# ScalarE's first-layer order pinned anew, and one weight group begun before the state sums, in a gated delta rule with a GELU layer pair

## The chip, the cores and the metric

The kernel runs on one core of a Trainium2 chip. Its engines are TensorE (PE: matrix products, and PEld: loading their weights), VectorE (DVE), ScalarE (ACT), GpSimd (POOL) and SyncE (SP, which issues most DMAs). The metric is the time of one execution on the device in microseconds; lower is better.

## The reference

The work is a delta rule over 768 positions, for 4 x 8 heads of 48, whose output is the input of two dense layers with an exact GELU between them. All arrays are float32, but `moe_w_in` and `moe_w_out` arrive as float64, which the kernel decodes itself.

```python
B, H, S, D = q.shape                      # 4, 8, 768, 48
k_n = k / (norm(k, axis=-1) + 1e-6)
for t in range(S):
    y[:, :, t] = q_t @ state
    v_old = state^T k_t
    state = state + beta_t * outer(k_t, v_t - v_old)
x = y.transpose(0, 2, 1, 3).reshape(B * S, H * D)      # 3072 x 384
h = x @ w_in                                           # 384 x 2048
g = 0.5 * h * (1 + erf(h / sqrt(2)))
out = g @ w_out                                        # 2048 x 384
```

## The kernel before

**Tiling.** The positions are cut into 12 chunks of 64. Within a chunk the recurrence is a triangular system, so that the state is touched once per chunk. A unit is one chunk of one pair of batches (`NA` = 2 units a chunk, 128 partitions: 2 batches x 64 positions, 8 heads). Two chunks make a group; its triangular systems are eliminated together on VectorE (`eliminate_steps`) and joined on TensorE (`join`, from the third chunk on `join_run`). A chunk then goes: products with the state (`against_state`, psK), `subtract` (VectorE makes W, ScalarE copies y), `solve` (psU, ScalarE copies U), `use` and `update` (psY and psS), `next_state` (VectorE adds psS to the state St), `read` (x), `turn` (x transposed, xT).

**The two layers.** `fc1(c, f)` makes one of 16 slices of the hidden layer of chunk c: three products into a PSUM tile psH (L784), then a GELU on ScalarE into G. For chunk 0 psH takes one of two buffers (tag "mlp"), so slice f + 2 waits until the GELU of slice f has read its own. `fc2` makes psO from G and w_out (L802). From chunk 2 on other forms of both layers are used, which the change does not touch.

**Decoding the weights.** A float64 weight comes as two 32-bit words. `w_in` is 8 groups (0 to 7) of 256 columns, `w_out` 8 more (8 to 15). For group n: `fetch` (three or two DMAs from SP into a staging buffer), `begin` (VectorE takes the exponent bits out, L231 or L234), `exponents` (ScalarE maps them: two Prelu instructions where `two_kinks`, among these groups 3 to 7, else one Relu; L237, or L875 where they go through `keep`), `mantissas` (VectorE, L251 and L253), `signed` (VectorE, L261, and L260 where there is one kink), which also issues the fetch of the group four (w_in) or three (w_out) further on. Slice f of the first layer needs group f // 2.

**What sets the order.** The beginning, up to `by_hand.close()`, is written in program order for all engines. It ends with group 2's decoding and `next_state` of chunk 0. The rest is a list of steps with marks: `plan` gives each step a number, `emit` calls them in the order of these numbers. In this part VectorE executes in exactly that order. On the other engines a scheduler places an instruction where it reckons it ready, except that instructions that went through `keep` (which records them at its own line, L875) keep the program's order among themselves. For chunk 0 the GELUs go through `keep`, and so do the exponents of groups 3 to 7 (`decode_in`); slice f has its mark at 1.0 + 0.031 (f + 0.5), about. `decode_in` gives each group four marks: begin, exponents, mantissas, signed.

**The squares.** `sum_of_squares(u, h)` squares the 48 key values of one head on ScalarE and adds them up in the same instruction (L328; the trace shows it as two records). There are 32, for chunks 2 and 3, with marks from 1.48 to 1.8. They do not go through `keep`. In the order that the scheduler makes of it, three of them stand before the first exponents of group 3 and the others between the exponents and GELUs of the first layer. GpSimd then takes the square root of the sums as a power (`prep`, L349), one instruction for each of the two chunks, and VectorE makes factors of them (`finish_both`, L301 to L305) once the weights are decoded, as the first step of the second group's elimination. ScalarE also scales V with the roots (`scale_head`, L371).

Of the kernel before, what the change touches and what calls it, by code (L numbers as in the profile page):

```python
# [15 lines left out]
ACT = mybir.ActivationFunctionType  # L16
# [3 lines left out]
def kernel(  # L20
# [28 lines left out]
    nc = tc.nc  # L49
    B, H, S, D = q.shape  # L50
# [52 lines left out]
    for c in range(NC):  # L103
        for a in range(NA):
            u = tiles[c, a] = Unit()
# [96 lines left out]
    def fetch(n):  # L202
        if n >= len(w_parts):
            return
        dst, src = w_parts[n]
        if n < n_in:
            raw = stage[:, n % NS * 2 * WG:(n % NS + 1) * 2 * WG]
        else:
            raw = slots[(n - n_in) % len(slots)]
        w_raw[n] = raw.rearrange("q (n w) -> q n w", w=2)  # L210
        raw = raw.rearrange("q (m n w) -> q m n w", m=dst.shape[1], w=2)
        for m in range(dst.shape[1]):
            nc.sync.dma_start(out=raw[:, m], in_=src[:, m])
# [4 lines left out]
    def two_kinks(n):  # L218

        return 2 < n < n_in or n > n_in and n % 2 == 0  # L220

    def high(e, dt):

        return e.bitcast(dt).rearrange("q (n w) -> q n w", w=2)[:, :, 1]

    def begin(n):
        e = su.tile([128, WG], U32, tag="w_e", name="w_e")
        raw = w_raw.pop(n)
        halves[n] = w_parts[n][0].rearrange("q m n -> q (m n)"), raw[:, :, 0], raw[:, :, 1], e
        if two_kinks(n):  # L230
            nc.vector.tensor_scalar(e.bitcast(I32), raw[:, :, 1].bitcast(I32), 20, -1,  # L231
                                    op0=ALU.arith_shift_right, op1=ALU.bitwise_and)
        else:
            nc.vector.tensor_scalar(e, raw[:, :, 1], 20, 0x7FF, op0=ALU.logical_shift_right,  # L234
                                    op1=ALU.bitwise_and)
# [12 lines left out]
    def mantissas(n):  # L248
        dst, lo, hi, e = halves[n]
        bits = dst.bitcast(U32)  # L250
        nc.vector.tensor_scalar(bits, hi, 0xFFFFF, 0x100000, op0=ALU.bitwise_and,  # L251
                                op1=ALU.bitwise_or)
        nc.vector.scalar_tensor_tensor(dst, lo, 2.0 ** -32, bits, ALU.mult, ALU.add)  # L253

    def signed(n):

        dst, lo, hi, e = halves.pop(n)
        scale = high(e, BF16) if two_kinks(n) else e.bitcast(F32)
        if not two_kinks(n):
            nc.vector.scalar_tensor_tensor(e, hi, 0x80000000, e, ALU.bitwise_and, ALU.bitwise_or)  # L260
        nc.vector.scalar_tensor_tensor(dst, dst, 2.0 ** -20, scale, ALU.mult, ALU.mult)  # L261
        after = n + (NS if n < n_in else len(slots))
        if (after < n_in) == (n < n_in):
            fetch(after)
# [12 lines left out]

    def decode_in():

        marks = {3: (0.986, 0.988, 0.99, 1.07), 4: (1.05, 1.06, 1.1, 1.155),  # L280
                 5: (1.14, 1.15, 1.19, 1.22), 6: (1.205, 1.215, 1.25, 1.28),
                 7: (1.265, 1.27, 1.33, 1.36)}
        steps = []
        for n, (a, b, c, d) in marks.items():
            steps += [(a, (begin, n)), (b, (exponents, n, keep)), (c, (mantissas, n)), (d, (signed, n))]
        return steps

    NW = len(w_parts)
# [2 lines left out]
    Ds, Gs, Nus, XMs, gms, ns = {}, {}, {}, {}, {}, {}  # L291
# [28 lines left out]
    def sum_of_squares(u, h):  # L320

        if "both" not in ns:
            n23 = wk.tile([128, 2 * NA, H], F32, tag="n0", name="n0", bufs=1)
            ns[2], ns[3] = n23[:, 0:NA], n23[:, NA:]
            ns["both"] = n23
        if h == 0:
            u.ksq = wk.tile([128, H, D], F32, tag="ksq", name="ksq", bufs=1)
        nc.scalar.activation(u.ksq[:, h], u.Kn[:, h, 0:D], ACT.Square,  # L328
                             accum_out=ns[u.c][:, u.a, h:h + 1])

    def norms(c):
        us = [tiles[c, a] for a in range(NA)]
# [386 lines left out]
    def next_state(u):  # L719
        if u.c < NC - 1:  # L720
            nc.vector.tensor_tensor(St[:, u.a], St[:, u.a], u.psS, op=ALU.add)
# [152 lines left out]
    def keep(fn, *args, **kw):  # L874
        tc.keep_in_program_order(fn(*args, **kw))  # L875
# [254 lines left out]
    exponents(2)  # L1130
    mantissas(2)
    signed(2)
    for u in first[:NA]:
        next_state(u)
    by_hand.close()
# [16 lines left out]
    def state_at(c, *times, first=(), second=()):  # L1152

        steps = state_steps(c, first, second)
        if len(times) > len(steps):
            steps = steps[:-1] + [(turn, tiles[c, a]) for a in range(NA)]
        return [(t, step) for t, step in zip(times, steps) if t is not None]

    plan = [at(c + 1 + 0.25 * (c == 1), c + 2 + 0.25 * (c == 0), ffn_steps(c)) for c in range(NC)]
    plan += [decode_in(), at(1.365, 1.9, decode_steps(n_in, NW)), at(1.91, 1.911, [(1.0, late)])]  # L1160
    rows1, join1 = eliminate_steps(1), join_steps(1)
    plan += [at(0.98, 0.985, [(1.0, load, 3)]),
             [(t, (join, 0, range(NA, 2 * NA), level)) for level, t in enumerate((1.085, 1.16))],
]
    sums = [(1.0, sum_of_squares, tiles[c, a], h) for c in (2, 3) for a in range(NA) for h in range(H)]
    plan += [at(1.48, 1.8, sums), at(1.81, 1.811, [(1.0, fn, c) for c in (2, 3) for fn in (norms, prep)]), at(1.9, 1.905, [(1.0, finish_both)]), at(2.725, 2.726, [(1.0, queries, third)]),
             state_at(1, 1.31, 1.4, 1.5, 1.56, 1.58),
# [125 lines left out]
```

## Time and profile before

| what | value |
|---|---|
| runs, us | 649.33, 651.1, 651.32 (median 651.1) |
| the profiled execution, us | 652.12 |
| its span, first to last instruction, us | 650.4 |
| mean granted TensorE clock | 0.981 |
| PE busy | 623.0 us, 96%, 9702 instructions |
| DVE busy | 499.4 us, 77%, 1023 instructions |
| ACT busy | 259.2 us, 40%, 586 instructions |
| POOL busy | 63.3 us, 10%, 58 instructions |
| one square, two records on ACT, ns | 230 and 188 (median), overlapping |
| one power on POOL, ns | 2914 (mean) |
| w_in DMAs from 54 to 72 us, issue to landing, us | 3.1 to 4.9, median 4.1 |

Times in the texts are microseconds from the start of the span, unless said otherwise. A timeline row gives start, duration, engine, line, operation, output <- inputs, shape, and in brackets the idle time of the engine before it and what ended that. "x6" is six records; a float32 product of TensorE shows as two records, so one slice of the first layer is six. A stage row gives the stretch, its length, then busy time (and records) of PE, PEld, DVE, ACT and POOL, the mean granted TensorE clock, the DMA engines' busy share, and GB/s. A busy TensorE is not TensorE at its peak[...].

### The profile page before, as it was taken

The page shows a single profiled execution, that of the slowest core. Times are in us where ns is not written, and L with a number is a line of the kernel's source. Part 1 is how long each engine was busy: PE and PEld are TensorE (multiplying, and loading weights), DVE is VectorE, ACT ScalarE, POOL GpSimd, SP SyncE. Part 2 cuts the span into 40 slices and gives each one's busy share as a digit, 9 for nine tenths or more (in the row PEclk, how much of TensorE's full clock was granted, in tenths as well). Part 3 has the DMA queues.
Part 4 walks back from the last instruction along what each step waited for, and adds up shares of the span by engine and source line. Part 5 has one row for each costly group of instructions (what it writes and reads, how often), then busy time and mean ns, then how long its engine had stood idle before and what let it go on. Part 6 is the DMA issues. An engine that isn't in the chain of part 4 may idle for free.

```text
span 650.4 us, 22163 instructions
## 1 busy us (share of the span) xinstructions
PE 623.0 (96%) x9702; PEld 575.8 (89%) x9702; DVE 499.4 (77%) x1023; ACT 259.2 (40%) x586; POOL 63.3 (10%) x58
## 2 busy tenths in 40 slices
PE   6767999999999999999999999999999999999997
PEld 5665777776799999999999999999999999999997
DVE  6999579998899997999767999667999665454342
ACT  3366875723453147133147133157133153132230
POOL 4042110100121003101003001004001000000000
PEclk9976799999999999999999999999999999999999
DMA  9795727211543235222325312312222400100101
GB/s 128 173 274 167 128 75 220 24 25 30 87 64 48 42 50 93 43 40 38 65 27 85 60 31 38 67 17 44 38 31 35 71 6 3 25 2 2 26 2 25
DMA packets 158433, 39.79 MB, mean 61 GB/s; under 512 B 150016, under 2 KB 153216, under 8 KB 158336
## 3 DMA queue, kind: packets, MB, share of 16 engines
q1 hardware_dynamic: 155344, 36.94, 29.8%
q10 hardware_dynamic: 2992, 1.43, 1.0%
q8 instruction: 76, 1.25, 0.8%
q14 instruction: 21, 0.17, 0.1%
HBM read 33.62 MB, written 4.72 MB: 59 GB/s over the span
## 4 chain that ended last, share of the span: by engine, by line
PE 83%; DVE 10%; ACT 3%; DMA 2%; issue 2%; SPq 0%; DVEq 0%; ACTq 0%
PE psX L832 12%; PE psY L887 11%; PE psY L832 8%; PE psX L887 8%; PE psO L802 6%; PE psV L887 5%; PE psZ L887 5%; PE psH L784 5%; PE psZ L832 4%; PE psV L832 4%; PE psK L658 3%; PE psG L412 3%; PE psJ L584 2%; DVE tmp L492 2%; DVE Nu L494 2%; PE psY L707 2%
## 5 line engine op out<-in xcount | busy, mean ns | idle before, releaser
L494 DVE TENSOR_TENSOR Nu<-Nu,tmp 128x30 f32<-128x30 f32 (+9 forms) x180 | 61.3, 341 | 6.2
L887 PE MATMUL psX<-xT,w_in_sb 128*128 128x128 f32 x480 | 64.6, 277 | 0.6 <-DVE p L984 0.5
L492 DVE TENSOR_TENSOR tmp<-Nu 128x30 f32<-128x30 f32 (+9 forms) x180 | 61.1, 340 | 4.7
L887 PEld LDWEIGHTS psX<-xT,w_in_sb 128*128 128x128 f32 x480 | 58.8, 192 | 2.0 <-issue 0.8
L875 ACT COPY xT<-psX 128x768 f32<-128x768 f32 x9 | 7.2, 798 | 124.4 <-PE psX L761 124.4
L832 PE MATMUL psX<-w_out_sb,G 128*128 128x192 f32 x320 | 55.3, 326 | 0.0
L784 PE MATMUL psH<-xT,w_in_sb 128*128 128x256 f32 x192 | 47.2, 401 | 5.1 <-ACT G L875 5.1
L832 PEld LDWEIGHTS psX<-w_out_sb,G 128*128 128x128 f32 x320 | 52.1, 190 | 0.0
L349 POOL TENSOR_TENSOR n<-n,half 128x16 f32<-128x16 f32 x10 | 29.1, 2914 | 230.4 <-DVE n L347 203.1
L784 PEld LDWEIGHTS psH<-xT,w_in_sb 128*128 128x128 f32 x192 | 37.6, 200 | 12.8 <-ACT G L875 6.7
L802 PE MATMUL psO<-w_out_sb,G 128*128 128x384 f32 x128 | 44.5, 493 | 0.0
L887 PE MATMUL psY<-xT,w_in_sb 128*128 128x128 f32 x320 | 42.3, 275 | 0.0
L875 ACT COPY pu<-psZ 128x512 f32<-128x512 f32 x40 | 23.4, 586 | 39.1 <-PE psZ L887 39.1
L887 PEld LDWEIGHTS psY<-xT,w_in_sb 128*128 128x128 f32 x320 | 38.9, 192 | 0.0
L802 PEld LDWEIGHTS psO<-w_out_sb,G 128*128 128x128 f32 x128 | 23.4, 190 | 14.1 <-DVE w_out_sb L261 0.5
L875 ACT ACTIVATE G<-G 128x512 f32<-128x512 f32 x40 | 25.2, 629 | 19.0 <-DVE G L918 18.1
L374 POOL TENSOR_TENSOR V<-V,n 128x384 f32<-128x384 f32 x18 | 16.6, 936 | 133.3 <-DMA V<-in_v_dram 55.4
L832 PE MATMUL psZ<-T,pu 128*128 128x192 f32 x160 | 28.6, 332 | 0.0
L832 PE MATMUL psY<-T,G 128*128 128x192 f32 x160 | 28.6, 332 | 0.0
L910 DVE TENSOR_TENSOR psY<-psY,pu 128x512 f32<-128x512 f32 x20 | 14.0, 698 | 18.0 <-PE psY L887 18.0
L832 PE MATMUL psV<-w_out_sb,G 128*128 128x192 f32 x160 | 27.7, 326 | 0.0
L832 PE MATMUL psX<-T,G 128*128 128x192 f32 x160 | 27.6, 326 | 0.0
(179 smaller groups left out, 1348.4 us busy)
## 6 DMA issues: line engine op xcount, KB each, us to landing
Kp<-in_k_dram SPq DMA_DIRECT2D x76, 96.0 KB, 3.4
w_out_sb<-in_moe_w_in_dram SPq DMA_DIRECT2D x24, 256.0 KB, 4.5
w_raw<-in_moe_w_out_dram SPq DMA_DIRECT2D x16, 384.0 KB, 5.2
V<-in_v_dram SPq DMA_DIRECT2D x48, 96.0 KB, 3.3
out_dram<-o_sb SPq DMA_DIRECT2D x36, 96.0 KB, 2.2
Qp<-in_q_dram SPq DMA_DIRECT2D x64, 32.0 KB, 2.3
Qp<-in_q_dram SPq DMA_DIRECT2D x16, 96.0 KB, 4.4
Qp<-in_k_dram SPq DMA_DIRECT2D x32, 32.0 KB, 2.4
```

The source lines that it names most:

```text
L349: nc.gpsimd.tensor_tensor(flat, flat, half, op=ALU.pow)
L374: engine.tensor_tensor(u.V, u.V, ns[u.c][:, u.a].unsqueeze(2).to_broadcast([128, H, D]), op=ALU.mult)
L412: nc.tensor.matmul(psG[HALF[p], r, i * NP + j, :], lhsT=u.Kt[rows, p, j, :], rhs=(u.Qt if x else u.Kt)[rows, p, j, :], start=True, stop=True)
L492: nc.vector.tensor_tensor(tmp, nu[:, j + 1:, j:j + 1].to_broadcast([128, n, j]), nu[:, j:j + 1, 0:j].to_broadcast([128, n, j]), op=ALU.mult)
L494: nc.vector.tensor_tensor(nu[:, j + 1:, 0:j], nu[:, j + 1:, 0:j], tmp, op=ALU.add)
L658: nc.tensor.matmul(u.psK[to, x, r, j, :], lhsT=(u.Qt if x else u.Kt)[rows, p, j, :], rhs=St[rows, u.a, p ^ r, j, :], start=True, stop=True)
L784: nc.tensor.matmul(psH, lhsT=w_in_sb[:, f // 2, m, f % 2 * 128:(f % 2 + 1) * 128], rhs=xTs[c][:, m, :], start=(m == 0), stop=(m == NM - 1))
L802: nc.tensor.matmul(u.psO, lhsT=G[:, u.a, f, :], rhs=w_out_sb[:, f, :], start=(f == 0), stop=(f == NF - 1))
L832: nc.tensor.matmul(ps_, lhsT=lhs[:, f, :], rhs=rhs[:, f, :], start=first and f == 0, stop=f == FH - 1, skip_group_check=not first)
L875: tc.keep_in_program_order(fn(*args, **kw))
L887: nc.tensor.matmul(ps_[:, i], lhsT=lhs[:, f // 2, f % 2 * 128:(f % 2 + 1) * 128], rhs=rhs, start=first and i == 0, stop=True, skip_group_c ...
L910: nc.vector.tensor_tensor(L1["Y1"], L1["Y1"], L1["pu"][:, 0], op=ALU.add)
```

## The change

Three edits, with no instruction added or removed.

1. `decode_in` has other marks. Exponents of groups 3 to 7 move to 1.03, 1.09, 1.18, 1.24 and 1.30, which puts each pair between two GELUs: after slice 0, 2, 5, 7 and 9. Before they stood at 0.988, 1.06, 1.15, 1.215 and 1.27: before slice 0, and after slices 1, 4, 6 and 8. Some begin, mantissas and signed marks move too.
2. `begin(3)` leaves that list and is called by hand after `signed(2)`, ahead of `next_state` of chunk 0, whose two additions to the state follow it on VectorE.
3. `sum_of_squares` goes through `keep`: the 32 squares keep their place in the program, behind the GELUs of chunk 0.

```diff
     def decode_in():
 
-        marks = {3: (0.986, 0.988, 0.99, 1.07), 4: (1.05, 1.06, 1.1, 1.155),
-                 5: (1.14, 1.15, 1.19, 1.22), 6: (1.205, 1.215, 1.25, 1.28),
-                 7: (1.265, 1.27, 1.33, 1.36)}
+        marks = {3: (None, 1.03, 0.99, 1.04), 4: (1.0, 1.09, 1.1, 1.13),
+                 5: (1.12, 1.18, 1.14, 1.2), 6: (1.19, 1.24, 1.21, 1.25),
+                 7: (1.245, 1.3, 1.29, 1.36)}
         steps = []
         for n, (a, b, c, d) in marks.items():
-            steps += [(a, (begin, n)), (b, (exponents, n, keep)), (c, (mantissas, n)), (d, (signed, n))]
+            if a is not None:
+                steps += [(a, (begin, n))]
+            steps += [(b, (exponents, n, keep)), (c, (mantissas, n)), (d, (signed, n))]
         return steps
...
-        nc.scalar.activation(u.ksq[:, h], u.Kn[:, h, 0:D], ACT.Square,
-                             accum_out=ns[u.c][:, u.a, h:h + 1])
+        keep(nc.scalar.activation, u.ksq[:, h], u.Kn[:, h, 0:D], ACT.Square,
+             accum_out=ns[u.c][:, u.a, h:h + 1])
...
     exponents(2)
     mantissas(2)
     signed(2)
+    begin(3)
     for u in first[:NA]:
         next_state(u)
     by_hand.close()
```

## The prediction

> **What bounds the kernel now.** I read the page first, then the waits between 58 and 98 us, the stage table (`busy of each engine by stretch`), and the timelines of TensorE and ScalarE there. On the page TensorE's row of slices reads 9 from the fifth slice (65 us) on. That hides two things in the start, up to 97 us: waits between slices, and products that are busy at half the clock.
>
> The timelines of the two engines in the first layer of chunk 0, TensorE first:
>
> ```profile
> 59.73 1.89 PE L784 MATMUL psH<-xT,w_in_sb 128*128 128x256 f32 x8
> 65.36 2.24 PE L784 MATMUL psH<-xT,w_in_sb 128*128 128x256 f32 x6 [3.75 <-ACT G L875]
> 67.53 1.92 PE L539 MATMUL psJ<-XM,G 32*32 32x32 f32 x64
> 69.38 4.59 PE L784 MATMUL psH<-xT,w_in_sb 128*128 128x256 f32 x12
> ...
> 75.03 2.86 PE L784 MATMUL psH<-xT,w_in_sb 128*128 128x256 f32 x12
> ```
>
> ```profile
> 62.21 0.94 ACT L875 ACTIVATE w_e<-w_e,lim 128x768 f32<-128x768 int32 x1 [3.23 <-DVE w_e L231]
> ...
> 63.27 1.14 ACT L875 ACTIVATE w_e<-w_e,lim 128x768 int16<-128x768 f32 x1
> ...
> 64.95 0.36 ACT L875 ACTIVATE G<-psH 128x256 f32<-128x256 f32 x1
> ```
>
> The first product (6 records, f = 0) is finished near 59.9, yet its GELU runs at 64.95: the two exponents of group 3 are pinned in front of it, and ScalarE waits 3.23 us for the begin of that group on VectorE. The third product needs the PSUM buffer that this GELU frees, so TensorE stands 3.75 us. The two rows of 12 records are the same work, 4.59 us and 2.86 us. The stage table says why: after the stall the granted clock (eighth column, PEclk) is 0.55.
>
> ```profile
> 61.50:65.40 3.90, 0.15 (x2) 0.04 (x1) 3.53 (x6) 3.19 (x13) 0.00 (x0) 1.00 0.99 251
> 65.40:73.00 7.60, 7.60 (x79) 6.01 (x80) 3.41 (x7) 5.39 (x29) 3.03 (x1) 0.55 0.89 163
> 73.00:97.20 24.20, 22.84 (x456) 18.66 (x454) 17.74 (x26) 19.86 (x61) 2.92 (x2) 1.00 0.37 82
> 97.20:119.00 21.80, 21.80 (x92) 15.37 (x92) 21.38 (x29) 10.84 (x20) 0.00 (x0) 1.00 0.57 164
> ```
>
> The waits from 58 to 98 us, who waited for whom, in total, times, longest:
>
> ```profile
> PE psH L784 <- ACT G L875: 5.1, 4, 3.7
> DVE XM L550 <- PE psJ L539: 4.1, 1, 4.1
> ...
> ACT w_e L875 <- DVE w_e L231: 3.2, 1, 3.2
> DVE w_in_sb L261 <- ACT w_e L875: 2.7, 3, 1.4
> ```
>
> So ScalarE's order holds both others: TensorE loses 5.1 us standing and 7.6 x 0.45 = 3.4 us to the clock; VectorE waits 4.1 us for the late join and 2.7 us for exponents that stand behind squares. From 97.2 on TensorE has no gap (21.80 of 21.80).
>
> [...] 3.75 us idle, then clock near 0.5 for some 7 us. [...] the trace has a ready GELU behind a waiting exponent. [...] The trace is mixed: L253 took 1.47 instead of 0.96 us beside GpSimd's V product (50.19 to 52.33), but 0.96 beside the power at 69.97. [...]
>
> **The change part by part.** The built order of both kernels differs in few places. SP's and GpSimd's queues are the same, item by item: no DMA is issued in another order. VectorE: begin of group 3 stands before the two state sums; group 7's mantissas before the W block (four instructions) instead of behind it. ScalarE: each GELU and each pair of exponents in the order of the marks; the 32 squares behind the first layer; the exponent of group 9 now before the six copies of U. TensorE: one or two small products moved.
>
> *Begin of group 3 earlier* costs nothing in work. 0.5 us (L231: 0.55) go before the sums, which end at 62.2 instead of 61.7. Behind them waits the join's PSUM buffer, wanted at 62.9. Its weights were fetched at 31 to 35 us, so it does not wait itself.
>
> *The order and the squares.* I replay the trace by hand, each instruction starting when its engine and its inputs are ready. Durations, start to start, from rows at full clock: product 1.56 (6 records), join 1.1, psK 2.0, psU 1.1, psY 2.1; VectorE L231 0.47, L251 0.59, L253 0.88, L261 0.88, so mantissas 1.47, join scaling 1.41, W block 2.1; ScalarE GELU 0.26 to 0.36, exponents 0.94 and 1.1 (2.0 a pair), Zf copies 1.1, U copies 1.95, square 0.225.
> TensorE: f = 0 ends 59.9, f = 1 61.3. GELU 0 runs at 60.1, so f = 2 starts at 61.3: the stall is gone, and with it the slow clock. Join 62.9 to 64.0, f = 3 and 4 to 67.1, join to 68.2, f = 5 to 9 to 76.0, psK to 78.0, f = 10 and 11 to 81.1. The GELUs free each buffer in time (GELU 6 at 72.6 for f = 8 at 72.9 is the tightest).
> VectorE: begin 3 at 60.7, sums to 62.15, mantissas 3 to 63.6, begin 4 to 64.1, signed 3 to 65.0 (exponents done 63.3), join scaling 66.4, mantissas 4 67.9, begin 5 68.3, signed 4 69.2, mantissas 5 70.7, begin 6 71.2, signed 5 73.1 (its exponents end at 72.2, behind the Zf copies and GELU 5), mantissas 6 74.6.
> Here the fetch of group 7 is late: it is issued by SP from 69.68 to 71.8, behind twelve other loads, in an order that does not change; its three DMAs landed 3.7 to 3.8 us after issue, so about 75.2. Begin 7 to 75.7, signed 6 76.6, mantissas 7 78.1, W block 80.2, signed 7 81.1, begin 8 81.6.
> ScalarE: y copies to 80.3 behind W, GELU 10 80.6, so f = 12 from 81.2 to 82.8, psU 83.9, f = 13 and 14 to 87.0. The exponent of group 9 waits for begin 9 (83.5), ends 84.5, then U to 86.45 and GELU 13 86.75. This pin puts U back by 0.6 us (psU is ready at 83.9), which f = 13 and 14 hide. f = 15 runs 87.0 to 88.5, psY 88.5 to 90.6: TensorE has no gap worth naming left.
> The second layer (psO) then starts at 90.6. Before it starts at 97.21: **6.6 us** earlier. With a landing of 4.9 us, the longest of the twelve w_in DMAs, begin 7 moves 1.1 us and the same chain gives 5.5. I take 6.1, the middle.
>
> *After that.* TensorE is dense to 160 us, so what arrives earlier ends earlier, if VectorE's decoding of w_out and ScalarE keep up. Both chains hang on psS and x, which move by the same amount. The 32 squares, 32 x 0.225 = 7.2 us, now lie here. ScalarE had gaps of 0.97, 1.11, 1.44, 1.60 and 1.93 us before its instructions from 100 to 111 us; by the built order the squares come as 2, 5, 6, 7, 6, then 5 and 1: 0.45, 1.1, 1.35, 1.6, 1.35 us. They fit, to 0.1. The five ahead of the second GELU of chunk 1 make it 1.2 us late, which costs TensorE about 0.15 through a PSUM buffer. The last square ends near 108.6, the power on GpSimd 2.9 us later at 111.6, and VectorE wants it at 119.03 - 6.6 = 112.4. I cost them at nothing; with that cover gone they cost up to 1 us. Beside the two powers L253 may stretch by 0.5 us each; the row at 69.97 shows none. Both ends stay in the range.
>
> **Sum.** The span goes from 650.4 to 644.3; the profiled execution took 652.12 (1.7 around the span), so 646.0. The median of the runs is 651.1, 1.0 below it; the same 6.1 us gives 645.0.
>
> **The rivals.** *Half the gain.* The clock falls anyway: TensorE still works in pieces in the 60s[...]. Against it: the replay leaves no gap over 0.3 us before 80. Price: the 3.4 us above; 651.1 - 6.1 + 3.4 = 648.4.
> *Slower.* The squares move ScalarE's work into the stretch where VectorE is the full engine (21.38 of 21.80 us from 97.2 to 119), each w_out group waiting for its exponent. If the 7.2 us fall in whole on that chain, and TensorE on it, the end is 651.1 - 6.1 + 7.2 = 652.2. It turns slower when more than 6.1 us of the squares, 28 of 32, stand before exponents already wanted. For it: the groups of squares fit the gaps to 0.1 us. Against: they do fit, and VectorE's next step hangs on an exponent only at L260 and L261.
> *Nothing.* The gain comes at 90.6 and is lost before 160, for TensorE has other work to fill in and a later chain (VectorE's elimination from 119, back to back) ends last: 651. Against: that chain starts from the decoding, which moves too.
>
> **How the numbers follow.** Forecast 0.78 (643.5 to 646.8: the terms 5.5 and 6.6, up to 1 us for squares and powers, and 1 us for the spread of the runs, 649.33 to 651.32). Half the gain 0.09, nothing 0.06, slower 0.07. About 0.3%, 2 us, is what a measurement of this kernel can tell from no change. Faster 0.87, within 0.06, slower 0.07. The range goes from 643.0 to 648.6, to take in the half gain.
>
> **What would show it.** Right: no wait of TensorE for a GELU over 1 us from 58 to 90; clock 1.0 from 60 on; the joins at about 63 and 67 (before 67.5 and 73.9); begin 7 as the first VectorE instruction that waits for a DMA; psO first at 90 to 92; then every row to 160 earlier by the same 6 us. Wrong: a clock of 0.5 after 62; VectorE waiting at L260 or L261 for exponents from 95 to 112; the factors (L301 of before) waiting for GpSimd; or a shift at psO that is gone at 160.

## The result, and the profile after

| | kernel before | kernel after |
|---|---|---|
| median of 18 runs each, us | 649.9 | 646.12 |
| the profiled execution, us | 652.12 | 647.82 |
| its span, us | 650.4 | 645.8 |
| median of the spans, us | 648.6 (41 runs, of the second measurement) | 644.1 (18 runs) |
| time outside the span, us | 1.7 | 2.0 |

The ratio of the means is 0.9944, with a 95% interval from 0.993 to 0.9958: 3.6 us faster (3.8 between the medians). One slow run of before, of 1246.54 us, is left out of the ratio. A second measurement gave 0.9926 (0.9906 to 0.9946). The prediction was 645.0, in a range from 643.0 to 648.6: right in the sign and the range, 1.1 us too low. The gain that it forecast was 6.1 us.

The timelines of TensorE, then ScalarE, in the kernel after (lines are two higher than before, so L786 is the first layer's product, L804 the second layer's, L877 `keep`):

```profile
57.64 4.53 PE L786 MATMUL psH<-xT,w_in_sb 128*128 128x256 f32 x18
62.10 1.20 PE L541 MATMUL psJ<-XM,G 32*32 32x32 f32 x64
63.23 2.86 PE L786 MATMUL psH<-xT,w_in_sb 128*128 128x256 f32 x12
66.02 1.20 PE L541 MATMUL psJ<-Zf,XM 32*32 32x32 f32 x64
67.15 7.14 PE L786 MATMUL psH<-xT,w_in_sb 128*128 128x256 f32 x30
...
80.55 1.56 PE L786 MATMUL psH<-xT,w_in_sb 128*128 128x256 f32 x6 [0.86 <-ACT G L877]
...
86.89 1.56 PE L786 MATMUL psH<-xT,w_in_sb 128*128 128x256 f32 x6 [0.92 <-ACT G L877]
...
90.40 1.56 PE L804 MATMUL psO<-w_out_sb,G 128*128 128x384 f32 x4
```

```profile
59.62 0.38 ACT L877 ACTIVATE G<-psH 128x256 f32<-128x256 f32 x1 [1.97 <-PE psH L786]
60.52 2.13 ACT L877 ACTIVATE w_e<-w_e,lim 128x768 f32<-128x768 int32 x2 [0.51 <-DVE w_e L231]
62.51 0.63 ACT L877 ACTIVATE G<-psH 128x256 f32<-128x256 f32 x2
```

Slices 0, 1 and 2 now stand in one row of 18 records without a wait for a GELU. Their first GELU runs at 59.62, as soon as its product is there, and the exponents of group 3 come behind it. The same stretches in the stage table (busy of PE, PEld, DVE, ACT and POOL, then the granted clock):

```profile
61.50:65.40 3.90, 3.90 (x78) 3.27 (x77) 3.80 (x7) 3.50 (x5) 0.00 (x0) 1.00 1.00 219
65.40:73.00 7.60, 7.47 (x93) 6.10 (x92) 6.93 (x11) 6.17 (x12) 0.00 (x0) 1.00 0.75 162
73.00:97.20 24.20, 22.31 (x400) 17.61 (x400) 19.69 (x30) 18.01 (x56) 0.00 (x0) 1.00 0.57 138
97.20:119.00 21.80, 21.76 (x84) 15.48 (x83) 20.93 (x36) 18.41 (x79) 8.57 (x3) 1.00 0.41 108
```

TensorE is busy for 3.90 us of the first stretch, against 0.15, and the clock is 1.00 in the second, against 0.55. The waits between 58 and 98 us:

```profile
PE psH L786 <- ACT G L877: 1.8, 2, 0.9
DVE w_e L231 <- DMA w_out_sb<-in_moe_w_in_dram: 1.5, 1, 1.5
...
DVE w_in_sb L261 <- ACT w_e L877: 0.5, 1, 0.5
```

TensorE's waits for GELUs fall from 5.1 to 1.8 us, VectorE's for exponents from 2.7 to 0.5, and its wait of 4.1 for the join is gone. A new one stands between them: VectorE waits 1.5 us for a DMA.

In the kernel before, the second layer's first row is:

```profile
97.14 1.56 PE L802 MATMUL psO<-w_out_sb,G 128*128 128x384 f32 x4
```

It now starts at 90.40, 6.7 us earlier, and VectorE's rows at 160 us are 6.8 earlier. About 0.6 of that was there before the change's place: VectorE's last step of group 2 stood at 59.05 against 59.70. At the end, only 4.6 is left, for between 162 and 168 the profiled execution of after lost 2.2 us again. The pause of TensorE there, and two windows (a window, here and below, is a stretch of 3.41 us; the changes of the granted clock in that profile lie on its edges):

```profile
163.57 0.43 PE L718 MATMUL psY<-U,Kp 64*64 64x48 f32 x11 [1.34 <-issue]
```

```profile
160.84:164.25 3.41, 1.79 (x73) 1.51 (x66) 3.31 (x8) 1.55 (x3) 1.67 (x1) 1.00 0.35 44
164.25:167.66 3.41, 3.41 (x7) 1.69 (x6) 2.63 (x6) 0.00 (x0) 1.23 (x1) 0.50 0.43 54
```

TensorE pauses 1.34 us in the middle of chunk 2's state update (for nothing that the profile names), is busy for 1.79 of 3.41 us, and gets half the clock for the next 3.41. Whether that belongs to the change was the first question.

### The profile page after: what moved, and what is told of

Same layout as the page of the kernel before. It is cut to its first block, busy times and chain, and to the rows that moved or that the text cites. A ratio compares the mean times of both kernels' runs of the same rounds, so it can differ in the third digit from the quotient of the medians.

```text
span 645.8 us, 22160 instructions
## 1 busy us (share of the span) xinstructions
PE 621.7 (96%) x9702; PEld 574.4 (89%) x9702; DVE 499.2 (77%) x1023; ACT 260.3 (40%) x586; POOL 63.4 (10%) x58
## 3 DMA queue, kind: packets, MB, share of 16 engines
q10 hardware_dynamic: 2992, 1.43, 1.1%
## 4 chain that ended last, share of the span: by engine, by line
PE 86%; DVE 8%; ACT 2%; issue 2%; DMA 1%; ACTq 0%; SPq 0%; DVEq 0%
PE psX L834 12%; PE psY L889 11%; PE psX L889 8%; PE psY L834 7%; PE psO L804 7%; PE psH L786 6%; PE psV L889 5%; PE psZ L889 5%; PE psZ L834 4%; PE psV L834 4%; PE psK L660 3%; PE psG L414 3%; PE psJ L586 2%; DVE tmp L494 2%; DVE Nu L496 2%; PE psU L690 2%
## 5 line engine op out<-in xcount | busy, mean ns | idle before, releaser
L877 ACT COPY xT<-psX 128x768 f32<-128x768 f32 x9 | 7.2, 799 | 124.3 <-PE psX L763 124.3
L804 PE MATMUL psO<-w_out_sb,G 128*128 128x384 f32 x128 | 46.4, 508 | 0.0
L786 PE MATMUL psH<-xT,w_in_sb 128*128 128x256 f32 x192 | 44.6, 386 | 1.9 <-ACT G L877 1.8
L786 PEld LDWEIGHTS psH<-xT,w_in_sb 128*128 128x128 f32 x192 | 36.1, 192 | 8.7 <-ACT G L877 2.9
L877 ACT COPY pu<-psZ 128x512 f32<-128x512 f32 x40 | 23.5, 587 | 39.2 <-PE psZ L889 39.2
L889 PEld LDWEIGHTS psY<-xT,w_in_sb 128*128 128x128 f32 x320 | 38.9, 192 | 0.0
L804 PEld LDWEIGHTS psO<-w_out_sb,G 128*128 128x128 f32 x128 | 24.1, 196 | 14.9 <-issue 1.7
L877 ACT ACTIVATE G<-G 128x512 f32<-128x512 f32 x40 | 25.2, 630 | 18.6 <-DVE G L920 17.8
```

The source lines that it names most:

```text
L786: nc.tensor.matmul(psH, lhsT=w_in_sb[:, f // 2, m, f % 2 * 128:(f % 2 + 1) * 128], rhs=xTs[c][:, m, :], start=(m == 0), stop=(m == NM - 1))
L804: nc.tensor.matmul(u.psO, lhsT=G[:, u.a, f, :], rhs=w_out_sb[:, f, :], start=(f == 0), stop=(f == NF - 1))
L889: nc.tensor.matmul(ps_[:, i], lhsT=lhs[:, f // 2, f % 2 * 128:(f % 2 + 1) * 128], rhs=rhs, start=first and i == 0, stop=True, skip_group_c ...
```

## The experiments

I count a kernel by two numbers: the median of its spans, and in its profile the start of the second layer (psO). In the 14 profiles of all kernels the time from that start to the end of the span lay between 553.2 and 556.6 us, so a shift there reaches the end, within 3.4 us by which single executions differ. Smaller differences are read from the median spans.

| kernel | exponents in new order | begin 3 early | squares pinned | psO starts | median span | ratio of the times |
|---|---|---|---|---|---|---|
| before | no | no | no | 97.14, 94.90, 94.02 | 648.6 to 648.9 | |
| begin alone | no | yes | no | 93.40 | 648.0 | 0.9988 (0.9976 to 1.0) |
| squares alone | no | no | yes | 94.53 | 646.3 | 0.9971 (0.9958 to 0.9983) |
| order alone | yes | no | no | 92.05 | 646.0 | 0.9949 (0.9932 to 0.9966) |
| squares free | yes | yes | no | 92.25 | 646.7 | 0.9959 (0.9943 to 0.9974) |
| begin late | yes | no | yes | 90.64 | 644.6 | 0.9935 (0.9914 to 0.9955) |
| after | yes | yes | yes | 90.40, 92.42 | 644.1, 644.3 | 0.9944, 0.9926 |

### One part alone

*Begin of group 3 alone.*

```diff
-        marks = {3: (0.986, 0.988, 0.99, 1.07), 4: (1.05, 1.06, 1.1, 1.155),
+        marks = {3: (None, 0.988, 0.99, 1.07), 4: (1.05, 1.06, 1.1, 1.155),
...
+    begin(3)
     for u in first[:NA]:
         next_state(u)
```

> The kernel before with only the begin of group 3 ahead of the state's sums. The exponents of group 3 still stand in front of the first GELU, but can start 1.45 us earlier (two sums of 0.72), so TensorE's wait of 3.75 us becomes 2.3. If the half clock follows any stall of that size: product of the second layer 1.5 us earlier, 648.4. If 2.3 us is too short for the clock to fall: 3.4 us more, 4.9 earlier, 645.0. Rival (nothing, the gain is eaten by exponents behind squares): 649.9.

TensorE's wait was 2.48 us and no half clock followed it. The second layer came at 93.40: 3.7 us earlier than in the first profile of before, but only 0.6 earlier than in the third, which lost nothing to the clock either (94.02). The median span is shorter by 0.6 too. Neither number of the theory was right: both started from the first profile. The rival's number, no gain (649.9), is nearest to the measured 649.7, and the interval reaches 1.0. Its reason is not shown: VectorE waits for exponents for 1.3 us in all here.

*The new marks alone*, with the begin of group 3 at 0.986 in the list and free squares.

```diff
-        marks = {3: (0.986, 0.988, 0.99, 1.07), 4: (1.05, 1.06, 1.1, 1.155),
-                 5: (1.14, 1.15, 1.19, 1.22), 6: (1.205, 1.215, 1.25, 1.28),
-                 7: (1.265, 1.27, 1.33, 1.36)}
+        marks = {3: (0.986, 1.03, 0.99, 1.04), 4: (1.0, 1.09, 1.1, 1.13),
+                 5: (1.12, 1.18, 1.14, 1.2), 6: (1.19, 1.24, 1.21, 1.25),
+                 7: (1.245, 1.3, 1.29, 1.36)}
```

> The kernel before with only the new marks; begin of group 3 stays behind the sums, and the squares are free again. My theory (the order of exponents and GELUs is nearly the whole gain): no TensorE wait over 1 us, clock 1.0 from 60 on, joins near 63 and 67; squares in front of exponents leave some of VectorE's 2.7 us of waits, but begin of group 7 waits for its DMA till 75.2 anyway, so the second layer starts 5 to 6 us earlier and the time is 646.4. Rival (the begin is needed with it): exponents of group 3 wait for begin 3 behind GELU 0 and hold GELU 1 and 2; gain 3, time 648.5.

There is no long stall, and the joins come at 62.59 and 67.30: so far the theory holds. One wait of TensorE is over 1 us (1.08), and the time, 647.8, is nearer to the rival's 648.5 than to the theory's 646.4 (2.6 us of gain in span). That the early begin is what is missing, the rival's reason, does not hold: with it and free squares the median span is 646.7 against 646.0 here. What is missing is the pin of the squares. VectorE's wait for an exponent of group 5 in this kernel:

```profile
74.43 0.96 DVE L261 SCALAR_TENSOR_TENSOR w_in_sb<-w_in_sb,w_e 128x768 f32<-128x768 f32 x1 [3.53 <-ACT w_e L877]
```

Six squares, the Zf copies and a GELU stand between the GELU at 68.88 and that exponent (72.21 here, 69.03 in the kernel after), and TensorE waits 1.08 and 0.75 us for GELUs behind squares.

*The pin of the squares alone.*

```diff
-        nc.scalar.activation(u.ksq[:, h], u.Kn[:, h, 0:D], ACT.Square,
+        keep(nc.scalar.activation, u.ksq[:, h], u.Kn[:, h, 0:D], ACT.Square,
```

> The kernel before with only the squares pinned behind the first layer's GELUs. The exponents of group 3 still stand first and wait 3.2 us, so TensorE's stall of 3.75 us and the half clock stay (theory: gain at the second layer 0 to 1.5 us from VectorE's 2.7 us of waits, time 649.2, no more than 0.3 percent from before). Rival (the squares were the main obstacle): over 3 us faster. Second rival (the squares are harmful where they go now): slower than before by up to 1 us.

2.3 us shorter in span, with the stall (2.07 us, clock 0.5 from 64.7 to 68.1) still there: more than my theory gave, less than the first rival, and the second (harmful) is excluded. VectorE's longest wait for an exponent is 0.25 us. So free squares were a cost of their own, about as large as the order's. Through which wait they cost it is shown only in part: VectorE waits for exponents for 0.5 us in all in this profile, against 2.7, 1.2 and 1.6 in the three of before, and squares no longer stand between the exponents of group 3 and the first GELU.

### One part undone

*Squares free* in the kernel after, then *begin late*.

```diff
-        keep(nc.scalar.activation, u.ksq[:, h], u.Kn[:, h, 0:D], ACT.Square,
+        nc.scalar.activation(u.ksq[:, h], u.Kn[:, h, 0:D], ACT.Square,
```

```diff
-        marks = {3: (None, 1.03, 0.99, 1.04), 4: (1.0, 1.09, 1.1, 1.13),
+        marks = {3: (0.986, 1.03, 0.99, 1.04), 4: (1.0, 1.09, 1.1, 1.13),
...
-    begin(3)
```

> The changed kernel with the squares not pinned: begin 3 ahead of the sums, new marks, squares free again. In the run with the new marks alone an exponent of group 5 stood behind squares and the Zf copies, and VectorE waited 3.53 us for it. Theory (squares in front of exponents are what the pin removes, begin 3 gives almost nothing): again a wait of VectorE over 2 us at L261 near 71 to 74, second layer at about 92, time 647.6, as with the new marks alone (647.8). Rival (the pin does nothing): 646.2.

> The changed kernel with the begin of group 3 back behind the two state sums (mark 0.986), squares pinned. Theory: exponents of group 3 now stand behind GELU 0, so the begin has 1 us to spare; VectorE does the same work in another order, the join comes up at the same time, begin 7 waits for its DMA as before; time within 0.5 us of the changed kernel, 646.3. Rival (the early begin is part of the gain): 647.5 or more, with a TensorE wait for a GELU between 61 and 64.

Both theories hold. With free squares VectorE again waits 3.66 us at L261 (74.63), and the span is 2.5 us longer than after's (the nine spans lie from 645.8 to 647.1, the median of after's at 644.1). With the begin late it is 0.4 longer, within the spread. By the median spans the order is worth 2.6 us alone and 1.7 on top of the pin, the pin 2.3 alone and 1.4 on top of the order, both together 4.0 to 4.3. These steps rest on 6 to 22 runs each, and most intervals of neighbouring kernels overlap, so that their sizes are rough. The early begin gave 0.6 alone, 0.4 on top of both and -0.7 with free squares: no effect that these runs tell from zero.

### Second and third profiles

These are the two kernels unaltered, once more.

> The changed kernel once more, unaltered, for a second profile of it. Open: TensorE's pause of 1.34 us near 163 us and the halved clock behind it (about 2 us). Theory A (it belongs to the new order, or to where the earlier start puts it): pause over 1 us and a granted clock of 0.5 from 164 to 167 again, and rows after 180 us only 4.6 us earlier than before. Theory B (chance of one execution): no half clock there, the shift of 6 to 6.8 us stays to the end, span about 643.8. Ratio 0.9935 to 0.995 in either.

Theory B, as to the clock: in the second profile of after, the pause is there (1.07 us), the clock stays at 1.00, the stretch at 162 to 168 loses 0.3 us. Its span did not follow: 645.6 and not 643.8, for the second layer started only at 92.42. The pause stands in all 14 profiles (0.71 to 1.43 us) and is not the change's; the half clock behind it showed in two of them.

> The kernel before, unaltered, for a second profile. If the stall and the half clock of the first layer belong to the kernel: TensorE's wait of about 3.7 us for the GELU at 62 to 65 us again, and one or two stretches of 3.4 us at half the clock behind it. If the half clock was chance: the wait, but a clock of 1.0 from 66 to 73, and a second layer that starts near 94 instead of 97.2.

> The kernel before for a third profile, for the half clock behind the stall, of which two executions showed 3.4 and 1.7 us lost. Theory (how many stretches of 3.4 us at half clock follow the stall is chance, and the first profile had caught a bad one): 0, 1.7 or 3.4 us lost between 64 and 74, and the second layer's start moves by as much (93.2, 94.9 or 97.1). Rival (it is always 3.4 and the second profile was the exception): 3.4 and 97.

The stall is always there (3.75, 4.29 and 2.99 us), but what follows is not: the three executions lost 3.4, 1.7 and 0 us to the clock, and one of the control below, with the same order, 5.1. So the change has a worth beside the clock: against the third profile, which lost nothing (94.02), the second layer of after is still 3.6 and 1.6 us earlier. The windows of the second and then of the third profile:

```profile
60.93:64.34 3.41, 0.00 (x0) 0.00 (x0) 3.03 (x6) 2.73 (x10) 0.00 (x0) 1.00 1.03 273
64.34:67.75 3.41, 2.98 (x12) 1.98 (x14) 0.47 (x1) 3.38 (x20) 0.00 (x0) 0.50 0.82 130
```

```profile
60.27:63.68 3.41, 1.52 (x7) 0.99 (x6) 3.22 (x6) 2.05 (x4) 0.00 (x0) 1.00 1.00 285
63.68:67.10 3.42, 2.32 (x58) 1.89 (x60) 0.96 (x1) 3.39 (x22) 0.00 (x0) 1.00 0.90 147
67.10:70.51 3.41, 3.41 (x46) 2.54 (x42) 2.89 (x5) 3.38 (x19) 1.11 (x1) 1.00 0.77 131
```

In the second, one window (3.41 us) has no product at all, and the next has half the clock. In the third, a window's edge cuts the stall: 1.52 us busy on one side, 2.32 on the other, and the clock stays. The windows of the first profile:

```profile
62.67:66.09 3.42, 0.73 (x3) 0.68 (x4) 2.39 (x3) 3.39 (x18) 0.00 (x0) 1.00 1.03 212
66.09:69.50 3.41, 3.41 (x69) 2.58 (x67) 0.00 (x1) 3.41 (x15) 0.00 (x0) 0.50 0.82 131
69.50:72.91 3.41, 3.41 (x8) 2.74 (x9) 3.31 (x6) 1.23 (x10) 2.94 (x1) 0.50 0.89 192
```

I chose these edges by the changes of the clock: within one execution all that I read lie a whole multiple of 3.41 us apart (in the first profile 59.26, 66.09 and 72.91), and their phase differs from one to the next (the clock fell at 66.09 in the first and at 64.34 in the second, 1.75 us apart).

### The fetch of group 7

The kernel after, with the eight loads of the fourth chunk behind that fetch in SP's queue, then the same edit in the kernel before as a control (mark 1.075):

```diff
-plan += [at(0.98, 0.985, [(1.0, load, 3)]),
+plan += [at(1.045, 1.046, [(1.0, load, 3)]),
```

> The changed kernel with the eight loads of k and q of the fourth chunk behind the fetch of weight group 7 instead of ahead of it in SP's queue; nothing else moved by hand. Theory (the late landing of group 7, 75.15 and 77.18 us in two executions, holds begin 7, the W block and so slice 12): group 7 is issued near 63 and lands by 69, begin 7 follows the mantissas of group 6 at 73.6, W starts when psK is done (near 76.5), and the second layer starts 1.5 us earlier than 90.40 in a quiet execution and 3 us earlier than 92.42 in the other: time 644.0, ratio to before 0.990. Rival (another wait stands right behind, or SP's loads come late for the squares): no gain, 646.2.

> Control: the kernel before with the eight loads of the fourth chunk behind the fetch of group 7, the same edit that made the changed kernel 1 to 1.6 us faster. Theory (group 7's landing is a bound only in the changed kernel; in the kernel before begin 7 stood at 79.6 behind exponents, over 4 us after the landing): no change, 650.2, ratio 0.998 to 1.002. Rival (the earlier fetch or the later loads help or hurt by themselves): 1.5 us or more from that.

VectorE's begin of group 7 in the two profiles of after, the first and then the second (where the profile names another load as the one that landed last; but the packets of group 7 ended at 76.16, 1.0 us before, as they ended at 74.26, 0.9 us before, in the first):

```profile
72.65 0.96 DVE L253 SCALAR_TENSOR_TENSOR w_in_sb<-w_out_sb,w_in_sb 128x768 f32<-128x768 uint32 x1
75.15 0.56 DVE L231 TENSOR_SCALAR w_e<-w_out_sb 128x768 int32<-128x768 int32 x1 [1.55 <-DMA w_out_sb<-in_moe_w_in_dram]
```

```profile
74.03 0.96 DVE L253 SCALAR_TENSOR_TENSOR w_in_sb<-w_out_sb,w_in_sb 128x768 f32<-128x768 uint32 x1
77.18 0.56 DVE L231 TENSOR_SCALAR w_e<-w_out_sb 128x768 int32<-128x768 int32 x1 [2.19 <-DMA Qp<-in_k_dram]
```

The fetch on SP, in the kernel after and then with group 7 fetched first:

```profile
69.66 1.51 SPq L213 DMA_DIRECT2D w_out_sb<-in_moe_w_in_dram  x3
```

```profile
63.12 1.85 SPq L213 DMA_DIRECT2D w_out_sb<-in_moe_w_in_dram  x3
```

TensorE with group 7 fetched first:

```profile
76.26 4.25 PE L786 MATMUL psH<-xT,w_in_sb 128*128 128x256 f32 x18
...
88.79 1.56 PE L804 MATMUL psO<-w_out_sb,G 128*128 128x384 f32 x4
```

The fetch is issued at 63.12 instead of 69.66, the wait at L231 is gone, slices 10 to 12 run in one row, and the second layer starts 1.6 us earlier: up to there as the theory had it, down to 0.1 us. The time did not follow: the theory had 644.0. The median span is 643.5 (after: 644.1 and 644.3), 0.6 to 0.8 us less, the ratio 0.991 (0.989 to 0.993). That is the best time of the study, 645.32 (645.33 with one edit more, below), but its interval touches after's, so that it is the faster of the two is likely and not shown. The control did not move, though its fetch too was issued earlier (63.22 instead of 69.68): 1.0001 (0.9986 to 1.0015). In the kernel before, begin 7 stands behind exponents (it runs at 79.56 with no wait, after an L261 that waited 1.45 us for ScalarE), and no DMA holds it. The change made this transfer a bound for VectorE.

### The exponent of group 9

In `decode_steps`, on the kernel after alone and then with the fetch:

```diff
             begin(n)
-            exponents(n)
+            if n != n_in + 1:
+                exponents(n)
...
+            if n == n_in:
+                steps += [(0.0, exponents, n_in + 1, keep)]
```

> The changed kernel with the exponent of group 9 behind the GELUs of slices 13 and 14 instead of ahead of the six copies of U; VectorE's order is the same. The prediction held that this exponent puts U back by 0.6 us and that slices 13 and 14 hide it; the trace shows TensorE waiting 0.92 us for the GELU of slice 13 behind U. Theory: U and that GELU come 0.9 us sooner, the wait before slice 15 goes to 0.1, the second layer starts 0.8 us earlier (89.6 against 90.4), time 645.4. Rival (the wait before slice 15 is hidden in the later work, or GELU 15 behind two exponents is late now): 646.2 or more.

> Both edits together on the changed kernel: group 7 fetched ahead of the eight loads, exponent of group 9 behind slice 14. Theory (two separate waits in a row on TensorE's path): gains add, second layer at 88.0 against 88.79 with the fetch alone, time 644.5, ratio to before 0.990. Rival (only one of them can be on the path): as with the fetch alone, 645.3.

TensorE of the kernel after with this edit (its lines are three higher again):

```profile
83.96 4.15 PE L789 MATMUL psH<-xT,w_in_sb 128*128 128x256 f32 x18
...
90.06 1.56 PE L807 MATMUL psO<-w_out_sb,G 128*128 128x384 f32 x4
```

Slices 13 to 15 now run in one row: the wait of 0.92 us is gone, the second layer starts 0.3 us earlier in an execution that reached slice 12 0.8 later (81.39 against 80.55), and the median span is 643.6, 0.5 to 0.7 shorter than after's. The ratio, 0.9922 (0.9904 to 0.9939), cannot be told from after's. With both edits, from slice 10 to the second layer it took 11.36 us, against 12.53 with the fetch alone and 14.17 in after, yet the median span is 643.6: the gains do not add. In that profile TensorE waits 1.06 us at 92.06 for the copies of x on ScalarE. These stand behind the second exponent of group 10 and two squares, and came later relative to TensorE, so the rival (one of them on the path) describes the outcome. That wait was seen in one execution.

## Why the prediction was right, and where it was off

**The chain up to the second layer was right** at the steps that set it (predicted, then measured in the first profile of after): joins at 62.9 and 67.1, 62.10 and 66.02; begin 7 at 75.2 behind its DMA, 75.15; the W block from 78.1, 78.08; slice 12 at 81.2, 80.55; U at 84.5, 84.50; second layer at 90.6, 90.40. No wait of TensorE for a GELU was over 0.92 us, and in none of the eight profiles with the new order did the clock fall between 62 and 90. The forecast "clock 1.0 from 60 on" was met in the first profile and missed in the second, where a half clock from before the layer lasted until 60.9. The closeness is in part luck. The start of before was misread by a little (97.21; the row says 97.14), and VectorE began its last step of group 2 at 59.05, 0.65 ahead of the 59.70 that the replay took from before. In the second profile the second layer came at 92.42, outside the 90 to 92.

**TensorE's own durations were too long in the replay.** It gave every slice 1.56 us, the length of a row of six records. In a longer row a slice takes 1.43 (2.86 for two in the prediction's own row at 75.03, 7.14 for five at 67.15 above). So slice 10 started at 76.23, where the replay had 78.0, and TensorE then stood for 0.86 us before slice 12. The sum came out right all the same, because the DMA and VectorE behind it set slice 12, not TensorE.

**The squares and the powers** cost nothing in this profile, as forecast. The second power ended at 111.73 (predicted 111.6) and the factors ran at 112.25 (112.4) with no wait; the powers took 3.17 and 3.48 us instead of 2.9. That left 0.5 us. L253 beside the second power took 0.96. The change made the kernel faster, and so did the pin of the squares alone, so the rival *slower* falls.

**Half the gain**, the clock falling anyway, falls as a mechanism: in these eight profiles it fell nowhere in the first layer. *Nothing* falls: the shift of 6.7 was 6.8 at 160.

**One statement was wrong**: that the pin of group 9's exponent is hidden by slices 13 and 14, with no gap left worth naming. Slice 15 waited 0.92 us for the GELU that stood behind U (0.83 in the kernel before), and moving that exponent away removed the wait. In the replay the long durations of slices 13 and 14 had filled this gap.

**The mis-sized term is the gain in the last line of the sum.** I forecast 6.1 us; it was 3.8 between the medians of the runs and 4.5 between the medians of the spans (648.6 - 644.1). In those 6.1 stood the 3.4 us of clock loss, and these belonged to one execution: the three profiles of before lost 3.4, 1.7 and 0. The median of the runs cannot gain what it has not lost, yet I took the same 6.1 us from it as from the profiled execution. How much of the difference this explains is not shown: the second profile of before lost 1.7 us less in the first layer, and its span was 650.4 all the same.

The time was only 1.1 us too low because two other errors helped, and that is luck. The 651.1 that I started from was a median of three runs; that of 18 is 649.9. And the forecast span of 644.3, for an execution like the profiled one, is near the median span of 644.1, but the two profiled executions of after spanned 645.8 and 645.6; it carries over the 553.3 us behind the second layer's start from the first profile, nearly the shortest of the 14. As a sum: from 645.0, 1.0 for the distance to the profiled execution that I subtracted, 0.3 for the time outside the span (1.7 before, 2.0 after), less 0.2 in the span, gives 646.1.

**The spread between the two profiles of after** is the landing of group 7, used at 75.15 and 77.18. The prediction varied the time from issue to landing (3.7 to 4.9 us) but held the issue fixed at 69.68. In the second profile the issue itself came at 71.16, as two pairs of the loads ahead of it took 2.15 and 2.60 us on SP instead of 1.27 and 2.30, and the weights were used 6.0 us later, against 5.5. TensorE was behind in that profile from the first join on (63.49 against 62.10, behind the half clock until 60.9), but VectorE was ready for group 7 at 75.0 and waited 2.19 us.

What stays open: what TensorE pauses for in chunk 2's state update, what decides whether a half clock follows a window and how long it lasts, and where the 0.3 us outside the span come from.

## What to carry to other kernels

On ScalarE, in the kernel before, a GELU whose product was finished near 59.9 ran at 64.95, behind pinned exponents that waited 3.23 us. Pin the order in which inputs come up, and put work with slack (here 7 us of squares) behind all that is urgent. When a change removes stalls, ask which transfer was late and unseen behind them (here that of group 7: VectorE waited 1.55 and 2.19 us for it), and look for it in the queue's order. A loss to the granted clock that stands in one profile need not stand in the next (3.4, 1.7 and 0 us in three of one kernel): take a second profile before it goes into a sum.

## What the runs showed that I had not expected

The prediction estimated, from one profile, that the slow clock goes when the stall goes. In the eight profiles with the new order that held, but neither the length of a stall nor the busy share of a window settled in these traces what the clock did next. The windows followed by half the clock were busy for 0.00, 0.21, 0.37 and 0.41 of 3.41 us in the first layer, and 0.52 and 0.54 in chunk 2's small products; windows of 0.41 and 0.45 in the first layer, and one of 0.63 in chunk 2 (2.15 us, group 7 fetched first), were not. The two of 0.41 were busy for the same 1.40 us: after a stall of 2.07 us that lay in one window up to its edge (squares alone) the clock fell, after one of 2.48 that an edge cut (begin alone) it did not. The half clock then lasted one window, two, or three (5.1 us lost, in the control), though TensorE was busy for 3.41 of 3.41 us in the second and third.

All 14 profiles also have a long half clock ahead of the first layer, while the weights are decoded: it begins between 38.9 and 45.7 us, lasts four to six windows and ends between 57.5 and 61.8. The windows just before it were busy for 0.35 to 0.78. It reaches into the first slices, in some executions further than in others, and it stands in both kernels.

The time outside the span depends on the kernel and hardly on the run: 1.67 to 1.79 us in every run of before, 1.99 to 2.10 in every run of after, 1.72 to 1.84 with group 7 fetched first.
